# Sums and maxima that reach K and Q without DRAM in the first pairs of an attention-to-MoE kernel, zero matmuls in TensorE's gaps, and one maximum for the last rows of two heads

## The chip, the cores and the metric

The kernel runs on one core of one Trainium2 chip. The metric is the device time of one execution in microseconds; lower is better. The kernel before takes 969.17 us, the median of three runs that lie between 969.14 and 969.28.

## The reference, cut to what matters

```python
def _attn_ref(q, k, v, s):                      # q, k, v: 4 x 8 x 576 x 64, s: 4 x 8 x 576
    scores = scale * np.matmul(q, k.transpose(0, 1, 3, 2))
    cum = np.cumsum(np.maximum(s, 0.0), axis=-1)
    bias = -(cum[:, :, :, None] - cum[:, :, None, :])
    scores = np.where(causal, -1000000000.0, scores + np.minimum(bias, 0.0))
    scores = scores - np.max(scores, axis=-1, keepdims=True)
    attn = np.exp(scores)
    attn = attn / (np.sum(attn, axis=-1, keepdims=True) + 1e-09)
    return np.matmul(attn, v)
...
    x = attn_out.transpose(0, 2, 1, 3).reshape(B * S, H * D)
    h = x @ w_in;  x = (h - np.tanh(h)) @ w_out              # first MoE, 2304 x 512 by 512 x 2048 and back
    h = x @ w_in2; return (h * np.clip(h + 3, 0, 6) / 6) @ w_out2
```

The 32 heads give 32 score matrices of 576 by 576. Two dense layers with 2304 tokens follow.

## The kernel before

**Attention** goes over 16 pairs of heads (`heads(p)`). Q and K of a pair come from DRAM with the 64 channels on partitions (tile `tq`). Each is split into a rounded part (`Q`, `K`, the tiles `firsts`, also written Q1 and K1 in the source) and a remainder (`Q2`, `K2`, the tiles `seconds`), so that float32r products keep the precision. Rows 64 to 67 of `Q` and `K` carry what is added to the scores: `K` rows 64 and 65 hold the cumulated sums (high and low part), against ones in `Q`; `Q` rows 66 and 67 hold minus the row maxima (high and low part), against ones in `K`. One matmul thus computes score, bias and maximum together.

For each head there are four steps on TensorE and its neighbours:
- `mx` (L479): scores with queries on partitions, 1856 columns in six matmuls, for the maxima only. They go to the tiles `wide` and `bank`.
- `rd` (L488): VectorE adds the causal mask `maskA` and reduces each tile to one column of `Mt`. The last of the five query tiles has 64 rows only and is reduced by itself, once for each head.
- `mf`, `mo`, `mi` (L513 to L517, then two DMAs at L256): VectorE splits and transposes the maxima, one DMA writes them to `mdram`, another reads them back as rows into `Q`.
- `st` (L572, transposed scores with keys on partitions, 15 matmuls), `ex` (L575, exp on ScalarE into `pt`) and `pv` (L603, product with V in 14 instructions).

The cumulated sums are made once for all heads at the start (`cum`, L369 to L374, on VectorE in `rb`). Those of head 0 go to `K` by two DMAs from `rb`; those of all the others go to `cdram` and come back pair by pair (`cu`).

**The order** is not written by hand. `Plan` holds every step as an op with an engine, an estimated duration, what it waits for and a due time made from the table `PRIO`; `schedule()` plays the ops through a model of the engines and DMA queue, and the code is then issued in that order. Each engine works through its own list strictly in that order. All DMAs of the kernel are issued by SyncE's queue (SP). At the start, VectorE and GpSimd also write the constant rows of ones (`prep_first`, L339 to L341).

**After the attention** the two dense layers take TensorE from about 210 us to the end (lines L828, L859 and L1120, L1196). Their weights come as 64-bit words and are converted on ScalarE and VectorE (`convert`, `rounded`). The first six of the sixteen weight chunks are converted during the attention, from the scores of head 1 on.

## Time and profile before

| | |
|---|---|
| median of the runs | 969.17 us |
| the profiled execution, its own time | 968.87 us |
| span of its instructions | 967.1 us |
| TensorE matmul busy | 946.1 us (98%), 5560 matmuls |
| VectorE / ScalarE / GpSimd busy | 670.0 (69%) / 467.9 (48%) / 160.7 (17%) us |
| DMA moved | 195.91 MB, mean 203 GB/s |

The page counts an engine as busy while an instruction runs on it. A busy TensorE says nothing of its speed: the same matmul can take twice as long in one stretch as in another, so durations of equal forms have to be compared as well. The chain of work that ended last is followed back from the end; where it goes through TensorE for nearly its whole length, time is lost only where TensorE stands idle or slow.

### The profile page before, as it was taken

Reading aid. Unit: us, or ns where it says so; the run is one execution under the profiler, and the core shown is the slowest. Engines: PE = TensorE matmul, PEld = TensorE weight load, DVE = VectorE, ACT = ScalarE, POOL = GpSimd, SP = SyncE. Lnnn points to the kernel's source line nnn. Section 1 sums busy time; section 2 is a strip of 40 time slices with the busy share of each in tenths; the row PEclk is TensorE's granted clock in tenths of the full one; section 3 lists DMA queues with packets and bytes.
Section 4 is the critical chain, followed back from the end, with each engine's and each line's share of the span. In section 5 each row is a group of like instructions: output and inputs, shape, how many; then the busy total and the mean of one; then the engine's idle time right before and its main releaser. Section 6 shows DMA issues by size and latency. Waiting matters only on the chain.

```text
span 967.1 us, 14956 instructions
## 1 busy us (share of the span) xinstructions
PE 946.1 (98%) x5560; PEld 838.7 (87%) x5560; DVE 670.0 (69%) x1107; ACT 467.9 (48%) x714; POOL 160.7 (17%) x106
## 2 busy tenths in 40 slices
PE   3999999999999999999999999999999999999998
PEld 3777777778878888998888888999999999999998
DVE  7887777759998667767766835555775567765763
ACT  2677667755444433444443433444454434544442
POOL 8344646520000000003322223000000000000000
PEclk9999999999999999999999999999999999999999
DMA  4656776676635356556455690765696657866562
GB/s 123 183 164 175 214 184 196 166 237 261 188 94 191 151 217 224 176 180 226 160 209 186 213 316 31 256 218 201 241 324 220 235 201 248 317 219 235 201 225 98
DMA packets 70521, 195.91 MB, mean 203 GB/s; under 512 B 11634, under 2 KB 20338, under 8 KB 69168
## 3 DMA queue, kind: packets, MB, share of 16 engines
q1 hardware_dynamic: 70448, 194.95, 61.3%
q8 instruction: 44, 0.72, 0.3%
q14 instruction: 29, 0.24, 0.1%
HBM read 143.75 MB, written 44.09 MB: 194 GB/s over the span
## 4 chain that ended last, share of the span: by engine, by line
PE 94%; DVE 3%; ACT 1%; DMA 1%; issue 0%; SPq 0%; DVEq 0%; ACTq 0%
PE bank L828 20%; PE bank L859 20%; PE pair L1196 19%; PE pair L1120 18%; PE bank L603 9%; PE bank L572 6%; PE wide L479 1%; DVE junk L488 1%; PE bank L479 1%; DMA Q<-mdram 0%; ACT w L776 0%; DVE f_w L1140 0%; DMA K<-rb 0%; SPq L440 0%; DVE rb L370 0%
## 5 line engine op out<-in xcount | busy, mean ns | idle before, releaser
L859 PE MATMUL bank<-gg,w 128*128 128x512 f32 (+1 forms) x960 | 234.3, 368 | 0.5 <-ACT gg L847 0.3
L828 PE MATMUL bank<-xx,w 128*128 128x512 f32 (+1 forms) x960 | 233.3, 368 | 0.0
L859 PEld LDWEIGHTS bank<-gg,w 128*128 128x128 f32 x960 | 170.1, 189 | 30.9 <-ACT gg L847 1.3
L828 PEld LDWEIGHTS bank<-xx,w 128*128 128x128 f32 x960 | 170.5, 188 | 30.3
L1120 PE MATMUL pair<-op_w,w 128*128 128x384 f32 x648 | 118.0, 334 | 0.6 <-DVE f_w L1140 0.6
L839 ACT ACTIVATE g<-bank 128x512 f32<-128x512 f32 (+1 forms) x80 | 44.5, 556 | 147.4 <-PE bank L828 124.2
L1196 PE MATMUL pair<-w,op_W 128*128 128x256 f32 x918 | 115.1, 283 | 0.0
L1120 PEld LDWEIGHTS pair<-op_w,w 128*128 128x128 f32 x648 | 112.5, 188 | 1.2 <-DVE f_w L1140 0.9
L603 PE MATMUL bank<-pt,vf 128*66 128x320 f32 (+4 forms) x448 | 112.6, 365 | 0.3 <-ACT pt L575 0.3
L1196 PEld LDWEIGHTS pair<-w,op_W 128*128 128x128 f32 x918 | 112.8, 192 | 0.0
L849 POOL TENSOR_TENSOR gg<-g,gg 128x512 fp32r<-128x512 f32 x32 | 47.5, 1484 | 345.0 <-ACT gg L847 307.9
L843 DVE TENSOR_TENSOR g<-bank,g 128x512 f32<-128x512 f32 (+1 forms) x80 | 50.9, 636 | 64.7 <-ACT g L839 64.0
L572 PE MATMUL bank<-Q,K 128*128 128x320 f32 (+9 forms) x384 | 94.2, 367 | 0.2 <-DMA Q<-mdram 0.2
L575 ACT ACTIVATE pt<-bank 128x512 f32<-128x512 f32 (+2 forms) x128 | 63.4, 501 | 43.4 <-PE bank L572 41.3
L572 PEld LDWEIGHTS bank<-Q,K 128*128 128x128 f32 (+1 forms) x384 | 65.3, 195 | 19.2 <-DMA Q<-mdram 0.6
L847 ACT ACTIVATE gg<-g 128x512 fp32r<-128x512 f32 (+1 forms) x80 | 47.0, 587 | 43.4 <-DVE g L843 35.0
L488 DVE CUSTOM_DVE_ANT_0 junk<-bank,maskA 128x512 bf16<-128x512 f32 (+2 forms) x96 | 45.0, 469 | 29.0 <-PE bank L479 21.6
L603 PEld LDWEIGHTS bank<-pt,vf 128*66 128x66 f32 (+1 forms) x448 | 51.8, 139 | 11.7 <-issue 1.6
L425 POOL TENSOR_TENSOR Q<-tq,Q 64x1152 fp32r<-64x1152 f32 (+1 forms) x17 | 42.4, 2494 | 60.1 <-PE bank L572 18.9
L488 DVE CUSTOM_DVE_ANT_0 junk<-wide,maskA 128x384 bf16<-128x384 f32 x64 | 41.8, 653 | 9.2 <-PE wide L479 4.6
L435 POOL TENSOR_TENSOR K<-tq,K 64x1152 fp32r<-64x1152 f32 (+1 forms) x17 | 42.8, 2520 | 23.2 <-DVE K L428 7.6
L1196 PE MATMUL pair<-w,op_B 128*128 128x256 f32 x342 | 44.1, 283 | 0.0
(305 smaller groups left out, 1299.5 us busy)
## 6 DMA issues: line engine op xcount, KB each, us to landing
w<-wdram SPq DMA_DIRECT2D x149, 512.0 KB
wdram<-cv SPq DMA_DIRECT2D x56, 512.0 KB
raw_c<-in_w_dram SPq DMA_DIRECT2D x11, 1024.0 KB
raw_b<-in_w_dram SPq DMA_DIRECT2D x11, 1024.0 KB
raw_a<-in_w_dram SPq DMA_DIRECT2D x12, 512.0 KB
vf<-in_v_dram SPq DMA_DIRECT2D x16, 330.0 KB
rb<-rdram SPq DMA_DIRECT2D x8, 576.0 KB
xdram<-xb SPq DMA_DIRECT2D x16, 288.0 KB
```

Source lines behind the costliest of these rows:

```text
L488: nc.vector.tensor_tensor_reduce(out=junk[0:rr, 0:w], in0=r(b)[0:rr, col : col + w], in1=maskA[0:rr, m0 : m0 + w], scale=1.0, scalar=-3.0e ...
L572: nc.tensor.matmul(o, w, x, start=(i == 0), stop=(i == len(mms) - 1))
L575: nc.scalar.activation(r(pt), r(b)[:, 0 : CW[c]], AF.Exp, scale=0.125)
L603: nc.tensor.matmul(r(po[bank])[0:DV, oc : oc + n], r(vf)[0:rr, j, hh, :], r(pts[c])[0:rr, col : col + n], start=(j == 0), stop=(bank == 0 ...
L828: nc.tensor.matmul(r(ps)[:, 0:w], wt[:, c, :], x(c)[:, 0:w], start=(part == 0 and c == 0), stop=(part == 2 and c == NCC - 1),)
L839: nc.scalar.activation(r(g)[:, 0:w], r(ps)[:, 0:w], AF.Tanh)
L843: nc.vector.tensor_sub(x, r(ps)[:, 0:w], x)
L847: gho = plan.op("ACT", vec_us(w, 1.2, 205), lambda: nc.scalar.activation(r(gh)[:, 0:w], r(g)[:, 0:w], AF.Copy), [m, to_gg], [g, gh], base)
L849: glo = plan.op("DVE" if beside else "POOL", vec_us(w, 0.96, 155) if beside else vec_us(w, 0.44, 160), lambda: (nc.vector if beside else n ...
L859: nc.tensor.matmul(r(acc[e])[:, 0:w], a[:, es], bb[:, 0:w], start=f, stop=l)
L1120: nc.tensor.matmul(bank(k)[:, l], w[hw][:, l, kc], r(x)[:, hx, kc], start=(i in (1, 5, 2) and j == 0 and kc == 0), stop=(j == 2 and kc == ...
L1196: nc.tensor.matmul(r(c[k])[:, m * 256 : (m + 1) * 256], r(x)[:, hx, l, m * P : (m + 1) * P], w[hw][:, l], start=(i == order[chain_first[k] ...
```

## The change

1. **Sums.** `s` and its sums are kept on partitions 64 to 95, ReLU goes to ScalarE, and the high part of head 0 is copied by VectorE straight into `K` (`crow`). Head 1 gets its high part by a DMA from `rb` (`cu0`), and the low parts of both follow by DMA (`cu1`). For pair 0 the maxima use the high part alone (65 rows).
2. **Maxima of pairs 0 and 1** (`TURN`). The order of the three maxima steps is turned round (256 and 128 columns first). VectorE writes ones and the split maxima as four columns (`split`), TensorE multiplies them with an identity, which turns them into rows (`rows`, 20 matmuls in all), and ScalarE copies these rows from PSUM into rows 64 to 67 of `Q` (`put`). `mo` and `mi` are gone for these pairs. The first scores step of a head waits for the first two query tiles alone.
3. **All other pairs.** The last 64 rows of both heads are put in one tile, one on partitions 0 to 63 and one on 64 to 127, and reduced in one instruction with a mask of its own (`maskB`). VectorE copies one column of 64 maxima to its place.
4. **Zero matmuls.** `warm` runs 10 matmuls of 512 columns on `maskA` as soon as that tile is there, and `fill` puts one of 256 columns for every 0.115 us that the planner sees TensorE idle, up to the first scores step of head 3. That makes 61. They hold one PSUM bank (`wb`) until then.
5. **Preparation.** K of pair 0 is rounded on ScalarE. The ones of the later `firsts` tiles come by DMA from those of the first. The first weight chunk is loaded from head 3's scores on, where it was head 1's.
6. **Tables and costs.** `PRIO` has new values, `EARLY` shifts single steps of the first pairs, and the planner's DMA rate and least matmul time change. So the order changes everywhere.

```diff
+TURN = (0, 1)
+WARM = 10
+PAIRT = [
+    [(0, 2, 384, 0), (2, 4, S, 384)], [(0, 3, 512, 0)], [(0, 1, 256, 0), (0, 0, 128, 256), (1, 0, 128, 384)],
+    [(1, 3, 512, 0)], [(1, 2, 384, 0)], [(1, 1, 256, 0)],
+]
...
-    "lq": -82.46, "q1": -19.46, "kh": -21.99, "k2": 46.29, "q2": 73.66, "ql": -97.67, "kl": 7.77, "cu": 15.04,
...
+FIRST_W = 3
+FILL_H = 3
...
-    DMA_US, DMA_KB_US, ISSUE = 1.6, 220.0, 0.55
+    DMA_US, DMA_KB_US, ISSUE = 1.6, 250.0, 0.55
...
-    cm = plan.op("DVE", 3.1, cum, [ls, pm0], prio=lead, name="cum", port=True)
-    co = plan.dma(cum_out, 144, [cm], prio=lead, name="cum_out", n=2)
...
+    sa = plan.op("ACT", 0.65, lambda: nc.scalar.activation(s_t, s_t, AF.Relu, scale=8.0), [ls], prio=lead - 30, name="relu")
+    cm = plan.op("DVE", 1.4, lambda: nc.vector.tensor_tensor_scan(
+        out=c_t, data0=c_t, data1=s_t, initial=0.0, op0=ALU.mult, op1=ALU.add), [sa, pk0], prio=lead - 29, name="cum")
+    cr = plan.op("DVE", 0.46, lambda: nc.vector.tensor_copy(c_row(0, 0), c_t[0:1]), [cm], prio=lead - 28, name="crow")
+    ch = plan.op("DVE", 0.46, lambda: nc.vector.tensor_copy(cp[0], c_t), [cm], prio=lead - 27, name="cumh", port=True)
+    cl = plan.op("DVE", 0.77, lambda: nc.vector.tensor_sub(cp[1], c_t, f32(cp[0])), [ch], prio=lead - 26, name="cuml")
+    cu0 = plan.dma(lambda: move(c_row(1, 0), cp[0][1:2]), 5, [ch, pk0], prio=lead - 25, name="cu0_hi")
...
+    wb = Buf(banks)
+    def warm():
+        for _ in range(WARM):
+            nc.tensor.matmul(r(wb)[:, 0:512], maskA[:, 0:P], maskA[:, 0:512], start=True, stop=True)
+    def fill(us):
+        for _ in range(int(us / 0.115)):
+            nc.tensor.matmul(r(wb)[:, 0:256], maskA[:, 0:P], maskA[:, 0:256], start=True, stop=True)
...
+                def split():
+                    m = r(mt)[:, hh, i0:i1]
+                    nc.vector.scalar_tensor_tensor(out=slot[:, i0:i1, 2], in0=m, scalar=-2.0, in1=m, op0=ALU.mult, op1=ALU.add)
+                    return nc.vector.scalar_tensor_tensor(
+                        out=slot[:, i0:i1, 3], in0=m, scalar=-1.0, in1=f32(slot)[:, i0:i1, 2], op0=ALU.mult, op1=ALU.subtract
+                    )
+                def rows():
+                    for i in range(i0, i1):
+                        nc.tensor.matmul(r(b)[0:4, (i - i0) * P : (i - i0 + 1) * P], slot[:, i], identr, start=(i == i0), stop=(i == i1 - 1), skip_group_check=True)
+                def put():
+                    nc.scalar.activation(r(b1)[0][64:68, hh, q0:q1], r(b)[0:4, 0 : q1 - q0], AF.Copy)
...
+                        for h, q0, n_q in ((hh, i * P, P),) if hh < 2 else ((1, 448, P), (0, 512, D)):
...
-            deps = [omi[x], oq2[x], ok2[x], oql[x], okl[x], pid]
+            low = [oq2[x], ok2[x], oql[x], okl[x], pmt] + (cu1 if p == 0 else [])
+            deps = [low + omi[hh][:1]] + [low + omi[hh]] * 3
...
-                fc, [part], PRIO["conv"] + 2 * fc + part, [st_done[1][0]], rawp, wyp)
+                fc, [part], PRIO["conv"] + 2 * fc + part, [st_done[FIRST_W][0]], rawp, wyp)
...
     for o in plan.schedule():
+        if o.eng == "PE":
+            if o.start < filled.start and gap and o.start - gap > 0.2:
+                fill(o.start - gap)
+            gap = o.start + o.dur
```

TensorE's list, its first rows before. The names `K_0_97` and `Q_0_96` are the rounded tiles of pair 0.

```order
L479 MATMUL wide<-K_0_97,Q_0_96 128x384
L479 MATMUL wide<-K_0_97,Q_0_96 64x128
L479 MATMUL wide<-K_0_97,Q_0_96 64x448
L479 MATMUL bank_65<-K_0_97,Q_0_96 128x512
L479 MATMUL bank_66<-K_0_97,Q_0_96 128x256
L479 MATMUL bank_66<-K_0_97,Q_0_96 128x128
```

The same place after, from the last matmul of `warm` on:

```order
L423 MATMUL bank_65<-maskA 128x512
L644 MATMUL bank_66<-K_0_97,Q_0_96 128x256
L644 MATMUL bank_66<-K_0_97,Q_0_96 128x128
L644 MATMUL bank_70<-K_0_97,Q_0_96 128x512
L644 MATMUL wide<-K_0_97,Q_0_96 128x384
L644 MATMUL wide<-K_0_97,Q_0_96 64x128
L644 MATMUL wide<-K_0_97,Q_0_96 64x448
L427 LDWEIGHTS maskA
L427 MATMUL bank_65<-maskA 128x256
```

Ten zero matmuls stand ahead of head 0's maxima, which come in turned order, and the first of fifteen of `fill` stands right behind them.

TensorE's list before, where the maxima of pair 1 (`K_1_99`, `Q_1_98`) meet the first scores of head 0:

```order
L479 MATMUL wide<-K_1_99,Q_1_98 64x448
L479 MATMUL bank_65<-K_1_99,Q_1_98 128x512
L479 MATMUL bank_66<-K_1_99,Q_1_98 128x256
L479 MATMUL bank_66<-K_1_99,Q_1_98 128x128
L479 MATMUL wide<-K_1_99,Q_1_98 128x384
L479 MATMUL wide<-K_1_99,Q_1_98 64x128
L479 MATMUL wide<-K_1_99,Q_1_98 64x448
L572 MATMUL bank_70<-Q_0_104,K_0_105 128x256
L572 MATMUL bank_70<-Q_0_96,K_0_97 128x256
```

And after, where pair 1's first maxima stand now:

```order
L738 MATMUL bank_73<-pt_0_115,vf_108 66x320
L644 MATMUL wide<-K_1_99,Q_1_98 128x384
L644 MATMUL wide<-K_1_99,Q_1_98 64x128
L644 MATMUL wide<-K_1_99,Q_1_98 64x448
L566 MATMUL bank_66<-identr,turn 4x128 x3
L738 MATMUL bank_73<-pt_0_117,vf_108 66x192
L738 MATMUL bank_73<-pt_0_117,vf_108 66x320
L707 MATMUL bank_70<-Q_0_104,K_0_105 128x256
L707 MATMUL bank_70<-Q_0_96,K_0_97 128x256
```

Before, both heads of pair 1 are through `mx` ahead of any scores; after, head 0's scores come first, and pair 1's first maxima stand between them and the rest of pair 0.

SyncE's list before, from the sums to the loads of pair 1:

```order
L440 DMA tq<-in_k_dram 64x576
L256 DMA Q_0_104<-Q_0_96 64x576 x2
L256 DMA K_0_97<-rb 1x16x36 x2
L256 DMA cdram<-rb 32x576 x2
L440 DMA tq<-in_q_dram 64x1152
L440 DMA tq<-in_k_dram 64x1152
```

And after, up to the sums of pair 1:

```order
L265 DMA Q_0_104<-Q_0_96 64x576
L265 DMA K_0_97<-rb 1x16x36
L265 DMA Q_2_100<-Q_0_96 2x1280
L672 DMA vf_108<-in_v_dram 128x660
L265 DMA K_0_97<-rb 1x16x36 x2
L265 DMA cdram<-rb 32x576 x2
L265 DMA Q_0_104<-Q_0_96 64x576
L496 DMA tq<-in_q_dram 64x1152
L496 DMA tq<-in_k_dram 64x1152
L265 DMA K_2_101<-Q_0_96 2x2x576
L265 DMA K_1_99<-cdram 2x2x576
```

Pair 1's loads were the 12th and 13th DMA of the kernel and are now the 19th and 20th; the ones, V and the second `Q2` copy went ahead of them.

## Rows read from the trace of the kernel before

**Rows 1.** Busy time by stretch: length, busy us (instructions) of each engine, clock, DMA
```profile
core 0: us, PE busy (x) PEld busy (x) DVE busy (x) ACT busy (x) POOL busy (x), PEclk, DMA share, GB/s
0.00:9.93 9.93, 0.01 (x1) 0.04 (x1) 7.24 (x10) 4.00 (x5) 6.96 (x22) 1.00 0.39 104
9.93:27.30 17.37, 12.62 (x42) 10.07 (x43) 14.50 (x49) 5.38 (x7) 14.68 (x12) 1.00 0.47 114
27.30:60.00 32.70, 32.06 (x189) 23.96 (x188) 27.37 (x88) 20.81 (x39) 10.79 (x5) 1.00 0.69 189
60.00:200.00 140.00, 140.00 (x839) 107.68 (x837) 99.55 (x309) 100.48 (x187) 79.14 (x35) 1.00 0.70 186
200.00:300.00 100.00, 99.52 (x448) 80.49 (x448) 84.98 (x114) 47.03 (x68) 1.69 (x3) 1.00 0.55 186
```

**Rows 2.** TensorE in order of time: start us, us, instruction, [idle before, releaser]
```profile
9.93 1.14 PE L479 MATMUL wide<-K,Q 66*128 66x384 f32 x3 [9.93 <-DMA K<-rb]
...
15.12 1.14 PE L479 MATMUL wide<-K,Q 66*128 66x384 f32 x3 [3.31 <-DVE MT L513]
...
21.42 1.17 PE L479 MATMUL wide<-K,Q 66*128 66x384 f32 x3 [1.37 <-DVE Mt L488]
22.39 0.63 PE L572 MATMUL bank<-Q,K 128*128 128x256 f32 x2
...
44.44 0.64 PE L572 MATMUL bank<-Q,K 128*128 128x256 f32 x2
```

**Rows 3.** Groups by form, one maximum matmul, 9.9 to 16 and 31 to 32 us
```profile
L479 PE MATMUL bank<-K,Q 66*128 66x512 f32 x1 | 0.6, 628 | 0.0
...
L479 PE MATMUL bank<-K,Q 66*128 66x512 f32 x1 | 0.4, 390 | 0.0
```

**Rows 4.** VectorE in order of time, the ones and the sums
```profile
3.07 1.02 DVE L340 MEMSET K<- 4x1152 f32 x1 [0.19 <-issue]
...
4.25 1.11 DVE L369 TENSOR_SCALAR rb<-rb 32x576 f32<-32x576 f32 x1
...
5.39 1.35 DVE L370 TENSOR_TENSOR_SCAN rb<-rb 32x576 f32<-32x576 f32 x1
6.77 0.45 DVE L373 CAST rb<-rb 32x576 fp32r<-32x576 f32 x1
```

**Rows 5.** Pieces of the chain that ended last: start us, us, what
```profile
8.03 1.65 DMA K<-rb
...
30.75 4.29 DMA Q<-mdram
...
41.22 1.16 PE bank L603 x6
...
47.36 0.42 PE bank L479 x3
...
51.62 2.07 PE bank L572 x15
...
904.17 58.32 PE pair L1196 x486
```

**Rows 6.** SyncE, GpSimd, ScalarE and VectorE in order of time, loads and use
```profile
8.73 1.39 POOL L425 TENSOR_TENSOR Q<-tq,Q 64x576 fp32r<-64x576 f32 x1 [2.11 <-DVE K L428]
...
9.66 0.52 SPq L440 DMA_DIRECT2D tq<-in_q_dram  x1
...
10.22 0.59 SPq L440 DMA_DIRECT2D tq<-in_k_dram  x1
...
13.44 1.16 ACT L419 ACTIVATE Q<-tq 64x1152 fp32r<-64x1152 f32 x1 [6.57 <-DMA tq<-in_q_dram]
...
14.73 1.16 ACT L431 ACTIVATE K<-tq 64x1152 fp32r<-64x1152 f32 x1
...
26.35 0.76 DVE L428 CAST K<-tq 64x1152 fp32r<-64x1152 f32 x1
...
29.00 0.75 DVE L488 CUSTOM_DVE_ANT_0 junk<-wide,maskA 64x576 bf16<-64x576 f32 x1
```

More of the change, by code (lines that the diff above doesn't have):

```diff
@@ L217, in schedule @@
                         n.left -= 1
-                        n.ready = max(n.ready, o.end)
+                        n.ready = max(n.ready, free["PE"] if o.eng == n.eng == "PE" else o.end)
                         if n.left == 0:
@@ L352, in prep_mask, with prep_maskB, prep_maskT @@
         )
+    def prep_maskB():
+        nc.gpsimd.memset(maskB, 0.0)
+        for x in range(2):
+            m = maskB[x * D : (x + 1) * D, 512:S]
+            nc.gpsimd.affine_select(
+                out=m, in_=m, pattern=[[-1, D]], compare_op=ALU.is_ge, fill=-1.0e30, base=0, channel_multiplier=1,
+            )
     def prep_ident():
         make_identity(nc, identb)
+        nc.gpsimd.tensor_copy(identr, identb)
+    def prep_maskT():
         nc.gpsimd.memset(maskT, 0.0)
@@ L401, with ones_of, put, shift @@
     xbs = [Buf(xbp) for _ in range(B)]
+    def ones_of(p):
+        if p == 0 or p >= NS1:
+            return [pk0] if p == 0 else []
+        t = lead + 8 + p + EARLY.get(("ones", p), 0.0)
+        def put(x):
+            ones = firsts[0][0][64:66]
+            move(firsts[p][1][66:68, :, 0:S] if x else firsts[p][0][64:66], ones[:, :, 0:S] if x else ones)
+        a = [plan.dma(lambda x=x: put(x), 10, [pq0], prio=t, name=f"ones{p}") for x in range(2)]
+        return [a[0], plan.op("POOL", 0.15, lambda: nc.gpsimd.memset(f32(firsts[p][1])[0:68, :, S:SP], 0.0), [a[1]], prio=t, name=f"zero{p}")]
     def heads(p):
         t0 = 2 * p * T
+        def shift(kind):
+            return EARLY.get((kind, p), 0.0)
         b1, b2, tq, vf = Buf(firstp), Buf(secondp), Buf(tqp), Buf(vfp)
@@ L446, in heads @@
[L446 to L450 removed]
+            lq_prev.append(lq)
@@ L501, in heads, with maxima @@
-        rd_done.extend(rds)
+            move(k1[64:66, :, 0:S], cdram[2 * p : 2 * p + 2].rearrange("a i s -> i a s"))
+        if p == 0:
+            ocu = [[cr], [cu0]]
+        else:
+            ocu = [[plan.dma(cu, 5, [al, co], [b1], t0 + PRIO["cu"] + shift("cu"), name=f"cu{p}")]] * 2
         omi = []
-        for i, a in enumerate(parts):
+        def maxima(i, a):
             n = a.stop - a.start
```

234 lines of the change are left out of this document (146 added, 88 removed), and 2 rows, old and new, of the table PRIO.

## The prediction

> **What bounds the kernel now.** Read the share of the chain by engine first, then the busy time by stretch, then TensorE in order of time. The page gives 94% of the chain to TensorE. By stretch, TensorE is busy for all of the 140 us from 60 to 200, with 839 matmuls, that is 0.167 us for each; from 200 to 300 it lacks 0.5 us [rows 1]. Nothing can be won in those stretches by relieving another engine. The loss stands at the start: TensorE is idle for 9.92 us up to 9.93, for 4.75 us of the next 17.37 and for 0.64 of the next 32.70, in all 15.3 us [rows 1]. The three large gaps are one wait for the sums' DMA into `K` (9.93), one for VectorE's split of the first maxima (3.31) and one for a maximum that frees a bank (1.37) [rows 2].
>
> The busy part of the start is slow too. The granted clock reads 1.00 there, yet one and the same 512-column matmul took 628 ns at about 11 us and 390 ns at 31 us [rows 3]; that is the lower of TensorE's two levels (1.2 and 2.4 GHz) up to about 27.3 us. The first 60 us hold 1 + 42 + 189 = 232 matmuls [rows 1]. At the later 0.167 us these are 38.7 us of work, so **21.3 us are lost at the start: 15.3 idle and about 6.0 to the slow clock.** What the change can give is a part of these.
>
> **The change part by part.**
>
> *Sums.* VectorE's last constant, the ones of `K`, ends at 3.07 + 1.02 = 4.09, and `s` had landed by 4.25 at the latest, since its first reader started then [rows 4]. After: ReLU on ScalarE is beside the ones, then the scan (1.35) and one copy of a row, by the nearest row 0.45, since the same length on 32 partitions took that [rows 4]: 4.1 + 1.35 + 0.45 and three small gaps make 6.1. If `s` lands only at 4.25 and ReLU takes as long as the copies of like length, 0.7, it is 6.8. I take **6.1**, since `s` is issued ahead of all else. So the first real matmul comes 3.8 us earlier than 9.93 [rows 2]. Before it there are only zero matmuls, which cost nothing there: TensorE has nothing else to do.
>
> *Maxima of pairs 0 and 1.* Now the split of head 0's maxima releases TensorE at 15.12, and the first scores follow at 22.39 [rows 2], 7.3 us later. That way, two DMAs, goes. In its place stand two small VectorE operations, a turn on TensorE and a ScalarE copy. What is late next? The first scores also need both `Q2` and `K2`, which GpSimd makes after the sums (6.5) in two operations of 1.39 [rows 6]: 9.3. TensorE's own list is later: it reaches the first scores at about 11.8, behind 25 zero matmuls (3.0), both heads' maxima (1.7), two turns and the waits below. The price of the 20 turning matmuls of 128 columns: not below half of a 256-column matmul, 58.32 / 486 / 2 = 0.06, and not above the mean of a maximum matmul, 0.42 / 3 = 0.14 [rows 5]. I take 0.09, so **1.8** (1.2 to 2.8).
>
> *Zero matmuls.* `fill` puts 61 of 256 columns in line. A 256-column matmul took 58.32 / 486 = 0.12 [rows 5]: **7.3 us**. They are no free filling: the list is strict, so they cost this even where the real matmul behind them could have gone. They are the largest term, and they say how much idle time the planner itself still sees.
>
> *Uncovered waits.* Two can be worked out. (a) Head 1's sums still go by DMA: issued behind VectorE's copy and the DMAs ahead at about 7.3, landed 1.65 later [rows 5], at 9.0 or a little after; TensorE's first 15 zero matmuls and head 0's maxima end at 8.75. That is 0.35. (b) Pair 1's loads are the 19th and 20th DMA now, 15 of them behind a wait for VectorE's ones of `Q` (end 2.9). At 0.6 an issue, by the two load rows [rows 6], the Q load goes out at 12.1 where it went at 9.66. Then it was used 3.8 us later (13.44) and K at most 4.5 us after its issue at 10.22 (14.73) [rows 6]. So Q is there at 15.9, K at 17.2, VectorE's copy of 0.76 [rows 6] ends at 18.0, and pair 1's first maxima can go. TensorE comes to that row at: 6.1, plus two heads' maxima (1.7), 27 zero matmuls (3.2), 7 turns (0.6), one head's scores (2.07) and ten of the fourteen products with V (1.9, at 1.16 for six) [rows 5], plus wait (a) and 0.5 for the clock: about 16.5. Behind it in the list stand the rest of head 0 and all scores of head 1, which can't go ahead. The wait is 1.5. Together **1.8** (0 if the loads land faster; 6 if both this wait and one more grow as the worst read-back of maxima, 4.29 [rows 5]).
>
> *Clock.* At the lower end 0, if it is up when the first maximum starts; at the upper end half of the time to 27.3, 10.6 us. The warm-up keeps TensorE at work from about 2 us on without a gap, and zero matmuls go on behind it, where before there were three gaps [rows 2]. I take **0.5**.
>
> *Last rows of two heads.* VectorE saves one reduction of 0.75 [rows 6] in each of 14 pairs and gains one tiny copy. TensorE has the same twelve matmuls and columns in a pair. Worth nothing: VectorE is busy for 99.55 of the 140 us under a full TensorE [rows 1]. Were TensorE not full, it would be worth at most 14 x 0.75 = 10.5 us. The mask `maskB` is written by GpSimd ahead of its `Q2` work and is in the 6.5 above.
>
> *Weights, tables, costs.* The first weight chunk starts some 6 us later, and VectorE has 40 us to spare up to 200 [rows 1]. From 200 to 300 it is busy for 85 of 100 us [rows 1], so there the cover is thin. I cost the new order there at 0: the gain is at most the 0.5 us that TensorE lacks, the loss is a rival.
>
> **The sum.** After, the loss is 6.1 + 7.3 + 1.8 + 1.8 + 0.5 = 17.5 us, against 21.3. **Gain 3.8.** The profiled execution's 968.87 (span 967.1 and 1.8 around it) becomes 965.1; the median lies 0.3 above that execution, so **965.4**.
>
> **The rivals.**
>
> *The clock stays low (slower than before).* Zero matmuls and short waits alternate, and the level doesn't rise before about 27.3, as now. For this speaks the trace itself: from 9.93 to 27.30 TensorE was busy for 12.62 of 17.37 us and stayed slow [rows 1, 3]. Against it: the warm-up has no gap, and once the level was up, 0.64 us of gaps in 32.70 did not lower it [rows 1]. Price: from 6.1 to 27.3 half the work is done, 10.6 lost; the waits vanish behind the slow matmuls. 6.1 + 7.3 + 1.8 + 10.6 = 25.8, 4.5 more than now: 973.7. It decides from a clock cost of 0.5 + 3.8 = 4.3 on, that is when the level rises later than 6.1 + 8.6 = 14.7 us. The Trainium skill (TensorE: Matmul & The Clock Gate, "A second HAM failure mode: psum-queue depth-cycling") says that an engine which idles briefly and often between groups of matmuls can swing between the two levels and pay each time; by that rule this rival is the outcome. The slow stretch up to 27.3 bears it out, the 140 us from 60 on show nothing of the kind.
>
> *The loads of pair 1 are later still (no change).* The list is strict, so each microsecond there is one of the end. V, the sums and Q2 go just ahead and share the DMA engines. With one wait like the read-back of 4.29 [rows 5] on top, 17.5 + 4 = 21.5: 969.4. Against it: these loads are 1.2 MB together, 6.4 us at the 189 GB/s of the later stretch [rows 1], and from 8.5 on that ends at 15, before the landings that I took.
>
> *The waits lie where the zero matmuls are (faster yet).* Then 1.8 and 0.5 go to about 0.3, and the turns cost 1.2: 6.1 + 7.3 + 1.2 + 0.3 = 14.9, gain 6.4: 962.8. For it: the zero matmuls stand where idle time is expected.
>
> *The transition.* VectorE, at 85% from 200 to 300, is late with a converted weight because the first chunks start later: 3 us, 968.4.
>
> **How the numbers follow.** Forecast 0.57, faster yet 0.17, loads later 0.13, transition 0.05, clock low 0.08. The range leaves out the clock's rival and the far half of the late loads' and takes in the turn's and the waits' bounds: 961.8 to 969.5. A measurement of this kernel tells 0.2%, 1.9 us, from no change: below 967.2 is faster, above 971.1 slower. Faster: the forecast and faster yet, and a share of the late loads' and transition's lower parts, 0.78; within: the rest of those two, 0.14; slower: the clock's rival, 0.08.
>
> **What would show it.** First maximum at about 6 us, released by VectorE; first scores near 11.8 instead of 22.39; the first scores of head 3 near 40 instead of 44.44 [rows 2]; a wait of 1 to 2 us of TensorE before pair 1's first maxima, near 17; a 512-column maximum at 390 ns from the second head on; from 60 us on 0.167 us a matmul as now. The forecast is wrong if zero matmuls take 0.2 us, if TensorE's waits before 40 us come to more than 4 us, or if TensorE is idle by over 1 us between 200 and 300.

## The result, and the profile after

The changed kernel takes 977.57 us (median of 6 runs, 976.25 to 981.83), the kernel before 969.13 us beside it: ratio 1.0087, 95% interval 1.0071 to 1.0104. It is **slower by 0.9%**, where 965.4 us and faster was forecast. The profiled execution took 981.14 us, at a span of 979.4; it is one of the longer ones, with a mean granted clock of 0.991 where the shortest has 0.996. The medians, here and below, leave out slow executions, of which there is one, of 1168.28 us, in k4_and_maxima_by_head.

The start came out nearly as forecast. TensorE of the changed kernel in order of time (start us, us, instruction, in brackets the idle time before it and what ended it), to be held against [rows 2]:

```profile
1.43 4.45 PE L423 MATMUL bank<-maskA 128*128 128x512 bf16 x10 [1.43 <-POOL maskA L362]
6.02 0.70 PE L644 MATMUL bank<-K,Q 65*128 65x256 f32 x3
7.00 1.81 PE L427 MATMUL bank<-maskA 128*128 128x256 bf16 x15
9.73 0.70 PE L644 MATMUL bank<-K,Q 65*128 65x256 f32 x3 [0.92 <-DMA K<-rb]
11.95 0.54 PE L707 MATMUL bank<-Q,K 128*128 128x256 f32 x2
...
13.79 0.50 PE L707 MATMUL bank<-Q,K 128*128 128x320 f32 x1
18.21 1.81 PE L707 MATMUL bank<-Q,K 68*128 68x320 f32 x5 [3.93 <-ACT Q L569]
...
48.54 0.40 PE L707 MATMUL bank<-Q,K 128*128 128x256 f32 x2
```

The first maximum starts at 6.02 and the first scores at 11.95 instead of 22.39. Then TensorE stops for 3.93 us, and head 3's first scores, forecast near 40, start at 48.54; before they started at 44.44. So the whole lead of 10.4 us is gone within 37 us. The busy time by stretch, with the columns of [rows 1], shows the rest:

```profile
9.93:27.30 17.37, 13.08 (x64) 8.94 (x64) 7.49 (x26) 6.41 (x13) 7.63 (x5) 0.71 0.56 144
27.30:60.00 32.70, 32.05 (x210) 24.53 (x208) 26.55 (x95) 21.15 (x38) 11.15 (x5) 1.00 0.58 156
60.00:200.00 140.00, 139.41 (x816) 102.35 (x814) 99.25 (x310) 96.98 (x183) 74.85 (x32) 1.00 0.72 185
200.00:300.00 100.00, 97.44 (x433) 77.19 (x433) 75.32 (x98) 47.45 (x71) 6.32 (x5) 0.97 0.57 183
...
15.00:20.00 5.00, 1.79 (x7) 1.49 (x7) 1.56 (x5) 1.13 (x3) 0.00 (x0) 0.63 0.71 174
20.00:25.00 5.00, 5.00 (x18) 3.17 (x17) 0.00 (x0) 3.62 (x5) 2.62 (x1) 0.50 0.32 68
25.00:30.00 5.00, 5.00 (x33) 3.86 (x31) 2.96 (x9) 3.35 (x7) 2.62 (x1) 0.85 0.34 107
200.00:205.00 5.00, 2.44 (x12) 1.49 (x11) 1.24 (x2) 2.27 (x5) 1.87 (x2) 0.90 1.02 238
205.00:210.00 5.00, 5.00 (x21) 4.24 (x20) 3.20 (x5) 1.19 (x2) 3.06 (x3) 0.50 0.72 236
210.00:215.00 5.00, 5.00 (x26) 3.29 (x25) 3.78 (x7) 2.72 (x6) 1.29 (x1) 0.92 0.00 0
```

Three things are new. The granted clock falls to 0.50 (1.2 GHz) for about 10.2 us: that is 5 us for 20 to 25, and of the stretches beside it the shares that 0.63 and 0.85 leave, 3.7 and 1.5. So it is down from 16.3 to 26.5, that is from 2 us before the end of the stop. It falls a second time from 204 to 211, for 6.8 us. And between 60 and 200, at full clock, 139.41 busy us hold 816 matmuls, 0.171 us for each; before it was 140.00 for 839, 0.167 [rows 1]. The second fall begins near the end of a second stop (201.9 to 204.5), on the last pair's copy `Q2`. TensorE's waits (us in all, times, longest):

```profile
PE bank L707 <- ACT Q L569: 3.9, 1, 3.9
PE bank L707 <- DMA Q<-Q: 2.6, 1, 2.6
PE bank L423 <- POOL maskA L362: 1.4, 1, 1.4
PE bank L644 <- DMA K<-rb: 0.9, 1, 0.9
```

**Where both stops come from.** The queue (SPq) and ScalarE around the first stop, in order of time:

```profile
12.42 0.59 SPq L496 DMA_DIRECT2D tq<-in_q_dram  x1
13.06 0.59 SPq L496 DMA_DIRECT2D tq<-in_k_dram  x1
13.76 0.75 SPq L265 DMA_DIRECT2D K<-Q  x1
...
17.73 0.69 ACT L569 ACTIVATE Q<-bank 4x320 fp32r<-4x320 f32 x2 [4.75 <-DMA K<-Q]
```

ScalarE's `put` writes head 0's maxima into rows 64 to 67 of pair 0's `Q`. It waits 4.75 us for a DMA that has nothing to do with it: the ones for pair 2's `K`, which `ones_of` copies out of rows 64 and 65 of that same `Q`. The copy must have read them before `put` overwrites them. It goes out at 13.76, right behind pair 1's two loads, and is done when `put` starts at 17.73. The planner has no edge for this; the wait comes only from the tiles. The queue at the second stop:

```profile
191.36 1.28 SPq L797 DMA_DIRECT2D rb<-rdram  x2
192.73 0.61 SPq L265 DMA_DIRECT2D Q<-Q  x1
```

The piece of the chain that ended last there (start us, us, what):

```profile
192.73 11.62 DMA Q<-Q
...
204.49 5.36 PE bank L707 x20
```

The last pair's `Q2` copy is issued right behind the two 576 KB copies that spread a batch's reciprocal sums, and takes 11.62 us to land.

**TensorE's time as a sum.** The table counts each matmul of a profiled execution from its own start to the next one's, less the time in which TensorE is idle; the sum ends at the start of the last matmul.

| us | before | changed | both repairs (below) | before with zero matmuls (below) |
|---|---|---|---|---|
| idle | 16.4 | 10.9 | 5.4 | 7.2 |
| zero matmuls, warm-up included | 0 | 11.3 | 10.9 | 17.2 |
| turns | 0 | 1.5 | 1.4 | 0 |
| attention (1120 matmuls) | 194.1 | 200.0 | 193.7 | 188.7 |
| dense layers | 751.7 | 751.0 | 750.6 | 751.9 |
| sum | 962.2 | 974.7 | 961.9 | 964.9 |

The attention's row is the surprise: with the clock up from 6 us on it should have fallen by some 5.5, as in the last column, and it rose by 5.9.

### The profile page after: what moved, and what is told of

It is laid out like the page before. It is cut to its first block, busy times and chain, and to the rows that moved or that the text cites. A ratio compares the mean times of both kernels' runs of the same rounds, so it can differ in the third digit from the quotient of the medians.

```text
span 979.4 us, 15117 instructions
## 1 busy us (share of the span) xinstructions
PE 964.1 (98%) x5651; PEld 843.8 (86%) x5651; DVE 662.0 (68%) x1097; ACT 472.6 (48%) x725; POOL 155.6 (16%) x106
## 4 chain that ended last, share of the span: by engine, by line
PE 93%; DMA 3%; DVE 2%; SPq 1%; issue 0%; ACT 0%; DVEq 0%; ACTq 0%
PE bank L996 20%; PE bank L965 20%; PE pair L1333 19%; PE pair L1257 18%; PE bank L738 8%; PE bank L707 5%; PE bank L605 1%; DMA Q<-Q 1%; PE wide L605 1%; DMA K<-cdram 1%; DMA sdram<-xb 0%; DVE junk L613 0%; DMA K<-Q 0%; SPq L265 0%; DVE turn L559 0%
## 5 line engine op out<-in xcount | busy, mean ns | idle before, releaser
L996 PE MATMUL bank<-gg,w 128*128 128x512 f32 (+1 forms) x960 | 210.2, 368 | 0.3 <-ACT gg L984 0.3
L965 PE MATMUL bank<-xx,w 128*128 128x512 f32 (+1 forms) x960 | 210.2, 368 | 0.0
L1257 PE MATMUL pair<-op_w,w 128*128 128x384 f32 x612 | 111.8, 334 | 0.0
L1333 PEld LDWEIGHTS pair<-w,op_W 128*128 128x128 f32 x882 | 108.1, 192 | 0.0
L738 PE MATMUL bank<-pt,vf 128*66 128x320 f32 (+4 forms) x448 | 106.6, 370 | 0.0
L1257 PEld LDWEIGHTS pair<-op_w,w 128*128 128x128 f32 x612 | 106.4, 188 | 0.1
L707 PE MATMUL bank<-Q,K 68*128 68x320 f32 (+9 forms) x384 | 79.3, 344 | 6.9 <-ACT Q L569 3.9
L707 PEld LDWEIGHTS bank<-Q,K 68*128 68x128 f32 (+1 forms) x384 | 62.4, 202 | 14.1 <-ACT Q L569 4.3
L613 DVE CUSTOM_DVE_ANT_0 junk<-bank,maskA 128x512 bf16<-128x512 f32 (+3 forms) x98 | 47.1, 480 | 19.8 <-PE bank L605 10.1
L491 POOL TENSOR_TENSOR K<-tq,K 64x1152 fp32r<-64x1152 f32 (+1 forms) x17 | 42.3, 2491 | 18.9 <-ACT pt L710 10.4
L1333 PEld LDWEIGHTS pair<-w,op_B 128*128 128x128 f32 x342 | 42.4, 192 | 0.0
```

The source lines that it names most:

```text
L613: nc.vector.tensor_tensor_reduce(out=junk[:, 0:w], in0=r(b)[:, col : col + w], in1=m, scale=1.0, scalar=-3.0e38, op0=ALU.add, op1=ALU.max, ...
L707: nc.tensor.matmul(o, w, x, start=(i == 0), stop=(i == len(mms) - 1))
L738: nc.tensor.matmul(r(po[bank])[0:DV, oc : oc + n], r(vf)[0:rr, j, hh, :], r(pts[c])[0:rr, col : col + n], start=(j == 0), stop=(bank == 0 ...
L965: nc.tensor.matmul(r(ps)[:, 0:w], wt[:, c, :], x(c)[:, 0:w], start=(part == 0 and c == 0), stop=(part == 2 and c == NCC - 1),)
L996: nc.tensor.matmul(r(acc[e])[:, 0:w], a[:, es], bb[:, 0:w], start=f, stop=l)
L1257: nc.tensor.matmul(bank(k)[:, l], w[hw][:, l, kc], r(x)[:, hx, kc], start=(i in (1, 5, 2) and j == 0 and kc == 0), stop=(j == 2 and kc == ...
```

## Experiments: the two stops and the clock

All ratios are against runs of the kernel before on the same chip, whose medians there were 969.4 to 970.0.

| run | median us | ratio, 95% interval |
|---|---|---|
| x1_ones_elsewhere | 975.15 | 1.0052, 1.0033 to 1.0072 |
| a2_second_repair_alone | 975.00 | 1.0054, 1.0039 to 1.0068 |
| x2_q2_before_sums (both repairs) | 967.77 | 0.9975, 0.9965 to 0.9984 |
| x4_no_fill (first repair, no zeros in line) | 978.16 | 1.0082, 1.0053 to 1.0110 |
| x5_repaired_no_fill (both, no zeros in line) | 976.52 | 1.0070, 1.0058 to 1.0083 |
| b2_before_with_zeros | 971.00 | 1.0010, 1.0000 to 1.0020 |
| b6_one_stop_in_before | 981.64 | 1.0116, 1.0099 to 1.0133 |

**x1_ones_elsewhere.** The theory: both stops, each with the low clock behind it, are the loss. The rival: the early waits are only traded for one another. The ones for pair 2's `K` are read from ones that nobody overwrites:

```diff
+            if p == 2 and x:
+                return move(firsts[p][1][66:68, :, 0:S], firsts[0][1][66:68, :, 0:S])
```

> The changed kernel with one source changed: the DMA that writes pair 2's ones into K reads them from rows 66 and 67 of pair 0's K, which nothing writes later, and no longer from rows 64 and 65 of pair 0's Q. The list of every engine stays as it is; the only wait that goes is that of ScalarE's second copy of head 0's maxima for this DMA. Theory A (a false dependency: this wait stops TensorE for 3.93 us at 14.3, and the clock falls to its lower level in answer, up to about 26 us): the wait goes, TensorE reaches pair 1's first maxima at 16 to 17 and waits there 1 to 2 us for pair 1's K (VectorE's copy ended at 18.1), the clock stays up, pair 1's first maxima come at 18.2 instead of 23.96, and the time falls by 5 to 7 us to 970.5 to 972.5. Rival B (the zero matmuls and the turned rows are the loss, the wait only moves to the next late transfer): the first scores of head 3 stay at 47 to 49 us and the time at 976 to 978.

The start came right: head 3's first scores at 41.57 instead of 48.54, and no low clock before 198. But the ratio fell from 1.0087 to 1.0052 only, by 3.4 us, and 975.15 lies outside both theories. TensorE's longest wait in this kernel shows where the rest stayed, and the busy time by stretch what followed it:

```profile
PE bank L709 <- DMA Q<-Q: 3.4, 1, 3.4
```

```profile
195.00:200.00 5.00, 1.81 (x9) 1.69 (x9) 0.83 (x2) 1.54 (x4) 2.77 (x2) 0.88 1.02 266
200.00:205.00 5.00, 5.00 (x17) 3.17 (x17) 4.46 (x5) 0.83 (x3) 3.42 (x2) 0.50 0.58 181
```

The second stop grew from 2.6 to 3.4 us, with 0.50 behind it again. TensorE reaches the last pair 7.1 us earlier (194.8 for 201.9), and the copy lands only 6.3 us earlier (198.2 for 204.5), so the wait for it is longer.

**x2_q2_before_sums and a2_second_repair_alone.** The second repair makes the two large copies wait for the last pair's `Q2` copy. x2 has it on top of x1, a2 has it alone:

```diff
...
+    q2_of[NPR - 1].next.append(spreads[B - 2])
+    spreads[B - 2].left += 1
```

> The kernel of x1_ones_elsewhere, and the two large DMAs that spread the normalising factors of the third batch are made to wait until the copy of the last pair's Q into Q2 is issued (a few lists change from there on, about 190 us). Theory A (the second stop of TensorE, 2.56 us at 202, is this copy: issued at 192.73 behind those two DMAs it landed 11.6 us later; and the clock falls for about 7 us after it): the stop goes, no lower clock near 205, another 4 to 6 us less, 965 to 968. Rival B (the DMA engines are simply full there and something else is late at the same place): the stop moves, the time stays within 1.5 us of x1.

> The changed kernel with the second repair alone: the last pair's Q2 copy is issued ahead of the two 576 KB copies of a batch's reciprocal sums, the copy of ones from pair 0's Q stays as the change has it. Theory A (both stops, each with the stretch of lower clock behind it, add up): the start keeps its stop of about 4 us near 14.3 and the clock of 0.5 behind it, 16 to 26 us; the stop near 202 and the 0.5 behind it go; 970.5 to 973, about 5.5 to 7 us below the changed kernel, so that the first stop is worth about 3 to 5 us against the run with both repairs (0.9975 of before). Theory B (the second stop only moves elsewhere, as after the first repair): 974.5 to 977.5.

With both, the kernel is faster than before by 0.25%, in theory A's range. TensorE of x2 in order of time at the place of the first stop, and then its longest waits:

```profile
13.79 1.28 PE L711 MATMUL bank<-Q,K 128*128 128x320 f32 x6
...
18.32 0.67 PE L647 MATMUL wide<-K,Q 66*128 66x384 f32 x3 [0.78 <-DVE K L484]
```

```profile
PE bank L423 <- POOL maskA L362: 1.4, 1, 1.4
PE bank L647 <- DMA K<-rb: 0.9, 1, 0.9
PE wide L647 <- DVE K L484: 0.8, 1, 0.8
PE wide L608 <- DMA K<-cdram: 0.6, 1, 0.6
```

No wait is left above 0.9 us but the one for the warm-up's mask, and the clock is up from 5.1 us to the end of the matmuls. The wait that was forecast at pair 1's first maxima, 1.5 us near 17, is there: 0.78 at 18.32. Against the changed kernel's 1.0087 the first repair alone gives 0.0035 of 969, that is 3.4 us, the second alone 0.0033, 3.2 us, and both give 0.0112, 10.9: more than the sum, though each is known to some 2 us only. In x1 the stop that is left grows, and the clock falls for it. In a2 it doesn't grow (3.6 us for 3.9), and the low clock by it lasts only some 3.5 us in the profiled execution, where the changed kernel, with the same list on TensorE up to there, had 10.2:

```profile
9.93:27.30 17.37, 13.48 (x82) 9.50 (x82) 8.92 (x31) 8.54 (x16) 8.20 (x5) 0.90 0.61 150
```

a2 missed its range (970.5 to 973) in the median, while its profiled execution, 972.14, the shortest, lay in it. What the longer ones lost has no trace but their mean clocks. Its six executions took 972.14, 973.16, 974.99, 975.00, 975.81 and 977.15 us at mean granted clocks of 0.998, 0.996, 0.995, 0.995, 0.995 and 0.993. One thousandth is about 1 us. So a stop gives a kernel not only a cost but a spread: how long the clock stays down differs between executions of the same list. The range of the changed kernel's runs, 976.25 to 981.83 at clocks of 0.996 to 0.991, goes the same way, though not in strict order; in x5 below, which loses in several places, time and mean clock don't go together.

**b6_one_stop_in_before.** Does a stop lower the clock, or does this list of work? The kernel before, with the last pair's `Q2` copy issued five places later and TensorE's list untouched:

```diff
-    for o in plan.schedule():
+    ops = plan.schedule()
+    late_q2 = next(o for o in ops if o.name == "q2_15")
+    ops.remove(late_q2)
+    ops.insert(next(i for i, o in enumerate(ops) if o.name == "xr0") + 1, late_q2)
+    for o in ops:
```

> The kernel before with one entry of the queue five places later: the last pair's Q2 copy goes out at about 196.7 us instead of 187.5. TensorE's list is word for word that of before. The scores that need the copy stood at 197.46, so TensorE stops there once, by 2 to 3.5 us, and nowhere else. Theory A (a stop of that size late in the attention also lowers the granted clock, and the low stretch costs half its length): the granted clock falls to 0.5 for 3.4 to 10 us, and the time rises by 4 to 8 us to 973 to 977.5, about twice the stop. Theory B (only the stop counts): clock at 1.00 throughout, 971 to 973.

The busy time of b6 by stretch, and its one long wait from 45 us on:

```profile
200.00:205.00 5.00, 0.72 (x3) 0.14 (x1) 0.95 (x2) 0.78 (x2) 2.69 (x2) 0.96 0.87 240
205.00:210.00 5.00, 0.87 (x4) 0.69 (x4) 0.00 (x0) 0.00 (x0) 0.00 (x0) 0.50 0.93 321
210.00:215.00 5.00, 5.00 (x19) 3.70 (x18) 0.00 (x0) 2.09 (x5) 0.00 (x0) 0.52 0.01 5
```

```profile
PE bank L572 <- DMA Q<-Q: 8.4, 1, 8.4
```

The mechanism is theory A's: one stop, one fall of the clock, none before. The size isn't. The stop was 8.4 us instead of 2 to 3.5, since the copy went out at 200.17 and landed only at 209.1, among the transfers of the batch. The time, 981.64, is 4 us beyond theory A's range. Of the 12.1 us that the median lost, 8.4 are the stop, and the low clock outlasts it by some 5.7 us, which cost about half of that. The profiled execution, 983.10, lost 2.6 us more at its start, where the clock rose late (last section).

**The zero matmuls: x4_no_fill, x5_repaired_no_fill, b2_before_with_zeros.** x4 is x1 and x5 is x2 without the 61 zero matmuls in line. b2 is the kernel before with a warm-up of 24 and with 134 of 128 columns in its three gaps.

```diff
...
             if o.start < filled.start and gap and o.start - gap > 0.2:
-                fill(o.start - gap)
+                pass
```

> The kernel of x1_ones_elsewhere without the 61 zero matmuls of the gaps; the ten of the start stay, all else is in the same order. Theory A (they cost their 6.8 us in full only where a real matmul could have gone; TensorE waits for VectorE and the DMAs most of that time anyway, and they keep the clock up): within 3 us of x1, in either direction, with the lower clock in a part of the first 45 us. Rival B (they are pure loss): 5 to 7 us faster than x1, with the clock up all the same.

> The kernel with both repairs without the 61 zero matmuls in line; the warm-up stays. They are left out, nothing else moves. Theory A (they buy the clock: without them TensorE stops at the waits that they fill, and the clock falls once or twice before 45 us): 6.7 us of them go, 1 to 3 us of waits come in their place and 4 to 8 us are lost to the lower level, 967 to 971 where the kernel with them stood at 0.9975 of before. Theory B (they are only cost in a strict list): 962 to 964, with the granted clock at 1.00 from 6 us on.

> The kernel before with zero matmuls alone: 24 of 512 columns as soon as the mask is there, 66, 28 and 40 of 128 columns in the three gaps of TensorE's list before the first scores (into columns of a bank that nothing else uses there). All else is in the same order. Theory A (about 6 us of the start are lost to the lower clock, and the zero matmuls raise it): the clock is up before the first maximum at 9.9, the stretch from 21.4 to 27.3 shrinks by about 3 us since VectorE and the DMAs set the pace before it, and the time falls by 2.5 to 4 us to 965 to 966.6. Rival B (the early stretch is bound by VectorE's reductions and the DMAs up to the steady state, whatever TensorE's clock): within 1 us of 969.1.

Without them x4 is 3.0 us slower than x1, at the edge of theory A; as it says, the clock is down in parts of the first 45 us (9.0 to 15.9 and 32.9 to 43.2). x5 is 0.95% slower than x2, about 9 us, more than either theory said. Busy time by stretch of x5:

```profile
9.00:23.00 14.00, 13.00 (x47) 8.93 (x48) 8.18 (x26) 6.96 (x13) 7.85 (x7) 0.51 0.71 178
23.00:36.50 13.50, 10.60 (x65) 7.42 (x63) 11.14 (x40) 9.16 (x15) 6.49 (x3) 1.00 0.64 148
36.50:47.00 10.50, 10.27 (x33) 7.40 (x34) 7.07 (x26) 2.39 (x5) 0.00 (x0) 0.51 0.35 91
```

It drops 6.5 us of zeros, gets 3.5 of waits in their place, and its attention takes 205.1 us instead of 193.7. In the kernel before the same device gives nothing, 1.2 us more where theory A had 2.5 to 4 less: the attention falls by 5.5 and the idle time by 9.2, but the zeros take 17.2. In these two kernels zero matmuls pay where they fill short waits, not where a long chain has to be waited for.

## Experiments: the order of the steady stretch

With both stops away the attention still takes 193.7 us of TensorE, 5.0 more than in before with zero matmuls, though waits are not in that row. Every head has the same 35 matmuls in all of these kernels, so matmuls in a stretch without waits can be counted. The busy time from 60 to 180 us (columns of [rows 1]) of before:

```profile
60.00:180.00 120.00, 120.00 (x722) 92.63 (x721) 88.37 (x287) 85.88 (x157) 66.48 (x29) 1.00 0.68 184
```

Of b3, which has the products in a row:

```profile
60.00:180.00 120.00, 119.96 (x709) 87.38 (x708) 89.50 (x280) 86.11 (x158) 66.34 (x29) 1.00 0.72 184
```

Of b5, which has the paired last rows:

```profile
60.00:180.00 120.00, 120.00 (x714) 90.81 (x713) 86.95 (x272) 86.06 (x160) 65.03 (x29) 1.00 0.74 190
```

Of b7, which has both:

```profile
60.00:180.00 120.00, 120.00 (x706) 88.38 (x705) 86.87 (x277) 86.06 (x160) 64.57 (x29) 1.00 0.74 194
```

And of x2, the changed kernel with both repairs:

```profile
60.00:180.00 120.00, 119.33 (x696) 87.60 (x695) 87.06 (x270) 82.06 (x154) 60.35 (x27) 1.00 0.76 188
```

A full TensorE does 722 matmuls in before and 696 in x2, which has one wait of 0.6 us there. What differs is the order: in before the products with V alternate with scores and maxima of other heads (231 changes between products and other work in its list), in the changed kernel whole heads of products and of scores stand in rows (101, and 103 in x2).

| run | median us | ratio, 95% interval |
|---|---|---|
| b3_products_in_a_row | 971.21 | 1.0015, 1.0004 to 1.0026 |
| b4_last_rows_alone | 977.08 | 1.0075, 1.0046 to 1.0105 |
| b5_last_rows_from_pair_4 | 972.37 | 1.0027, 1.0016 to 1.0038 |
| b7_row_order_and_last_rows | 972.01 | 1.0026, 1.0016 to 1.0037 |
| g4_steady_order_back | 974.75 | 1.0063, 1.0038 to 1.0087 |
| k4_and_maxima_by_head | 973.70 | 1.0036, 1.0023 to 1.0048 |
| k5_start_with_old_order | 968.93 | 0.9996, 0.9987 to 1.0004 |
| s1_order_fewer_waits | 969.38 | 0.9997, 0.9988 to 1.0006 |

**b3_products_in_a_row.** The planner's one line of the change, put alone into before:

```diff
-                        n.ready = max(n.ready, o.end)
+                        n.ready = max(n.ready, free["PE"] if o.eng == n.eng == "PE" else o.end)
```

> The kernel before with one line of the planner changed as the change has it: after an op on TensorE the next op on TensorE that needs it is ready when the engine is free, not a latency later. All else (start, maxima, table, costs) is that of before. The line alone turns the steady order: the four products with V of a head, which stood between scores and maxima of other heads (231 changes between products and other work), now stand in one row of seven instructions (67 changes). Theory A (this order costs TensorE time without any gap: in the steady stretch of the kernel with both repairs TensorE spent 5.99 us on a head and in before 5.83, with no waits in either): 31 heads by 0.15 to 0.2 us, 973.5 to 975.5, TensorE busy for all of 60 to 200 and its mean distance of matmuls up from 0.167 to about 0.172. Theory B (the steady loss comes from something else, waits of other engines or the pairing of last rows): 968.5 to 970.5.

The order turns as described, TensorE has no wait from 60 to 180 us, and it does 709 matmuls instead of 722. The attention takes 196.8 us instead of 194.1, 2.7 more. The time rises by 1.2 to 1.5 us, less than theory A's 4 to 6. So the order costs something, but not all of the 5. Counted from 60 to 180 us, from a matmul's start to the next one's, a product with V takes 0.197 us on average where it took 0.143, while scores (0.176 for 0.205), maxima (0.155 for 0.185) and masks take less; the sum is some 2% more.

**b4_last_rows_alone, b5_last_rows_from_pair_4, b7_row_order_and_last_rows.** b4 is before with the paired last rows from pair 2 on, b5 from pair 4 on with a late mask, b7 is b5 with b3's line. The core of b5 (`both` as in the change):

```diff
-        for hh in range(2):
...
+        if p > 3:
+            rds = both()
+        for hh in range(2) if p < 4 else ():
```

> The kernel before with part 3 alone: from pair 2 on the last rows of two heads stand in one tile and are reduced at once with a mask of its own. Start, table and planner's costs are those of before; 205 changes between products and other work instead of 231. Theory A (the pairing is worth nothing, as predicted, VectorE stands under a full TensorE): 968.8 to 970.8. Theory B (all twelve maxima of a pair come due at once and this costs the steady stretch its 4 to 5 us): 972.5 to 975.

> The kernel before with the paired last rows from pair 4 on; the mask for them is made late, so that the start stays that of before up to the 131st instruction of TensorE. Theory A (pairing by itself costs TensorE 1 to 1.5 us of attention work, as the two runs with the steady order back differ, and the +7.3 of the earlier run with pairs from 2 on came from its start and its stop): 970 to 971.5, attention work 195 to 196 us where before has 194.1. Theory B (worth nothing): 968.8 to 970. Theory C (the pairing brings the late stop with it): clock of 0.5 after 180 us and 973 or more.

> The run before this one with the planner's one line for an op behind another on TensorE as well: products with V in a row and paired last rows together, on the start of before. Theory A (the two costs add up and explain the 5.0 us of attention work between both repairs, 193.7, and before with zeros, 188.7): attention work 197.5 to 199 where before has 194.1, 972 to 974. Theory B (one of them alone, or neither): 970 to 971.5.

b4 fell outside both theories: its list has a stop of its own before the last pair (0.6 and 0.2 us near 193), the clock is at 0.5 from 195.6 to 202.4, and its early heads come later. b5 keeps the start and has no stop: 714 matmuls instead of 722, and 2.8 us more, a little above theory A's 0.5 to 2; its attention takes 198.0 us, above theory A's 195 to 196, of which 2.6 are a later rise of the clock in the profiled execution. b7 has 706. In TensorE's attention work the two costs add in part: 13 and 8 matmuls fewer make 21, measured 16; the attention takes 198.3 us, 4.2 above before. In the time they don't: b7 is 2.5 us above before, no more than b5, since it has 0.7 us less idle time and 0.5 less in the dense layers than before, where b5 has 0.9 and 0.8 more. The pairing that I had priced at nothing because VectorE is not the bound costs TensorE, whose list it rearranges.

**g4, k4, k5, s1: giving the old order back.** All four take x2 and use before's table and rule from some pair on (g4 and k4 from 4, k5 and s1 from 5; k4, k5 and s1 with maxima by head too; s1 with fourteen due times moved). The core:

```diff
-                        n.ready = max(n.ready, free["PE"] if o.eng == n.eng == "PE" else o.end)
+                        n.ready = max(n.ready, free["PE"] if o.eng == n.eng == "PE" and t < 45.0 else o.end)
...
+        PRIO = PRIO_STEADY if p >= FROM else PRIO_FIRST
```

> The kernel with both repairs (ones from elsewhere, Q2 ahead of the sums; 967.77) with the table of before for pairs 4 and on, and before's rule for an op behind another one on TensorE from 45 us on. The first 232 instructions of TensorE, the 61 zero matmuls among them, stand as they did. 183 changes between products and other work where there were 103 (231 in before). Theory A (the order of the products costs 4 to 5 us there): about six tenths of that come back, 964.5 to 966, and the stretch from the first scores of head 3 to the end of the attention takes 166 to 168 us instead of 169.8 (165.0 in before). Theory B (the loss lies elsewhere): 967 to 968.5.

> The same kernel with the maxima of each head by themselves from pair 4 on, as in before (one reduction more in a pair). 201 changes between products and other work. Theory A (pairing is worth nothing by itself): within 1 us of the run with the steady order back, 964 to 966.5. Theory B (pairing costs TensorE's order or delays the scores): 2 to 3 us faster than that run, about 962.

> The kernel with both repairs; from pair 5 on it has before's table and before's maxima of each head by themselves, and from 45 us on before's rule for an op behind another on TensorE, so that products, maxima and scores alternate again (187 changes between products and other work; 103 with both repairs alone, 231 in before). The first 328 instructions of TensorE stand as they did. Summed over the whole run, TensorE's work of the attention took 193.7 us with both repairs, 191.8 with the order back and pairs kept, and 188.7 in before with zero matmuls. Theory A (order, pairing and stops hold the rest): 189 to 191 here, waits after 45 us under 2 us, 963.5 to 966 and 2 to 4 us faster than with both repairs alone. Theory B (another order brings its own waits, as the order back with paired maxima did): waits of over 3 us or a clock of 0.5 after 45 us, 968 to 972.

> The same kernel with another table from pair 5 on (fourteen due times moved by a few units), in which GpSimd, ScalarE and the queue give their results earlier; 189 changes between products and other work. Theory A: as the run before this one or up to 1.5 us faster, 962.5 to 965.5, TensorE without a wait of over 0.5 us between 45 and 205 us. Theory B: one of the waits before the last pair's scores stays, the clock falls behind it, 967 to 971.

TensorE's work fell as theory A says: 191.8, 192.2, 190.8 and 191.1 us of attention against 193.7. The time did not: g4 and k4 fell outside both theories, k5 and s1 in the times of theory B without the waits that it names. The old order, which has no waits of TensorE from 60 to 180 us on the old start, has them on the new one in g4, k4 and k5. g4 was idle for 1.96 of the 40 us from 100 to 140, k4 stopped on `Q<-mdram` for 2.8 us in two waits and its clock fell at 205.9. g4's executions fall into two groups, six of 972.7 to 975.5 us at mean clocks of 0.998 to 1.000, and four of 979.5 to 981.2 at 0.992 to 0.994; its profile is of the first. k5 waits from 45 us on:

```profile
PE wide L657 <- DMA K<-cdram: 1.0, 1, 1.0
PE bank L756 <- ACT stage L779: 0.8, 1, 0.8
```

k5 gains 2.9 us of attention on x2, but has 3.4 us more of idle time and 1.4 more in the dense layers: within 0.1% of before. s1 shows that these waits are not all: from 45 to 205 us TensorE waits for 0.3 us at most, as theory A asked, and the attention takes 2.6 us less than in x2, yet it is no faster. It has 1.5 us more in the dense layers and 1.7 more of idle time, most of that behind the attention:

```profile
PE bank L1022 <- ACT gg L1010: 1.3, 2, 1.1
```

Why the dense layers take longer behind the old order, no run shows. x2 stays the best kernel of the study.

## Why the prediction was wrong, point by point

- **Sums, first maximum, turns, zero matmuls: right.** 6.02 us for 6.1; 61 zero matmuls 6.8 us for 7.3, by 0.11 each; turns 1.5 for 1.8; first scores 11.95 for 11.8.
- **Uncovered waits: wrong in kind.** I took 1.8 us (0 to 6); up to 60 us they came to 5.9. Wait (a) is 0.92 for 0.35, wait (b) 0.78 at its place once the stop is repaired. But 3.93 were a wait that I hadn't looked for. I had read part 5 as "the ones come by DMA" and costed what these copies deliver. They also read a row that ScalarE then overwrites. The step "of a step that is moved, every wait counts" was done for what is produced, not for what is read.
- **Clock: the failed step.** I took 0.5 us, with an argument that began "once the level was up". It rested on 0.64 us of gaps in 32.70 [rows 1], the longest of 0.34. One stop of 3.93 brought 1.2 GHz back for 10 us, one of 2.56 for 7. The price is read from the changed kernel and x2, whose lists on TensorE are the same up to 194 us: 200.0 less 193.7 us of attention, **6.3**. My rival "the clock stays low" named the right resource, with 10.6 for the whole start, and the wrong mechanism: the level rose in time and then fell. The Trainium skill (TensorE: Matmul & The Clock Gate, "A second HAM failure mode: psum-queue depth-cycling") speaks of frequent short idling between groups; in these traces the falls stand at one stop or a few, and the many short waits of x2, none above 0.9 us, brought none. My reading of the level from one form, 628 ns against 390 [rows 3], was weak. That before's clock was low up to 27.4 is borne out by b2, whose clock is up from 7.4 us on but for 3.4 us and whose attention takes 5.5 us less. But the changed kernel has the same form at 634 ns between 28 and 60 us, at a granted clock of 1.00, so the sign "390 ns from the second head on" couldn't tell the level:

```profile
L644 PE MATMUL bank<-K,Q 66*128 66x512 f32 x2 | 1.3, 634 | 0.0
```

- **New order and last rows at 0: wrong by 5.0 us** (193.7 less 188.7), with the waits left out of both. "TensorE has the same twelve matmuls and columns" was true and not enough: the same matmuls take longer in another order. b3 and b5 show about 2.7 and 1.3 of it, the latter after taking 2.6 off for b5's later rise of the clock; b7 shows most of the sum. About 1 us stays open; the new table and the planner's new costs, which no run takes alone, may hold it.
- **From 200 to 300 us:** I had set the price for VectorE being late; what came late was a DMA, 2.56 us.
- **Signs and range.** Two of my three signs of being wrong came: waits of over 4 us before 40 us, and a stop of over 1 us between 200 and 300. The range's lower end, 961.8, doesn't come out of the bounds that I gave: turns at 1.2, waits and clock at 0 make 962.5. Nothing here hangs on it.

Put together on the profiled execution, 16.0 us above the forecast for it: waits up to 60 us 4.1, idle time after that 2.3, clock 5.8, order and pairing 5.0, less 0.9 for zeros, turns and first maximum and 0.7 for the dense layers: 15.6.

What speaks for the forecast's core: with two edges repaired, the same start makes the kernel faster than before, 0.9975, though not by the 3.8 us that I had worked out, since the order takes back its share.

## What to carry to other kernels

A change that lets TensorE arrive earlier has to be followed to the next thing it can run into: list for each new copy what it reads, not only what it writes, and for each large DMA what stands behind it in the queue. Price a stop at its length and half of the low-clock stretch that outlasts it, if there is one, and look for that stretch in the granted clock by windows of a few us, where the mean of the whole run (0.991) hides it. On an engine that is full, count its instructions in a stretch before and after: the same work in another order is not the same time.
